# Key slots of 64 in every batch, the first batch loaded ahead of both weights, and a two-way list order, in a fused sliding-window attention and two-layer projection

## The chip, the core and the metric

The kernel runs on one core of one Trainium2 chip. The time is the device time of one execution in microseconds (us). Five engines work beside one another, each on its own queue of instructions in a fixed order: TensorE (PE, with its weight loads as PEld), VectorE (DVE), ScalarE (ACT), GpSimd (POOL) and SyncE (SP). SP and, here, ACT issue the transfers (DMA).

## The reference

```python
# q, k, v: (8 batches, 8 heads, 576 positions, 64); w_in (512, 2048); w_out (2048, 512); all float32
scores = (1.0 / np.sqrt(64)) * np.matmul(q, k.transpose(0, 1, 3, 2))
rel = pos[:, None] - pos[None, :]
mask_plain = (rel >= 0) & (rel < 32)                      # heads 0 to 3
mask_dil = (rel >= 0) & (rel < 128) & (rel % 4 == 0)      # heads 4 to 7
attn = softmax(np.where(mask, scores, -1e9))
x = np.matmul(attn, v)         # heads side by side: (8 * 576 tokens, 512)
h = x @ w_in
out = np.maximum(0.01 * h, h) @ w_out
```

A query sees 32 keys: its own and the 31 before it, or every fourth of the 128 before it. In residue order (positions 0, 4, 8, ..., then 1, 5, 9, ...) a dilated head's 32 keys stand next to one another.

## The kernel before

**Attention.** A *visit* is two heads of one batch, a *unit* is a part of a visit: three units a visit (`unit`, L695 on), so 12 per batch and 96 in all. Scores (L726, L742) multiply a slot of 128 neighbouring keys with 96 queries of both heads, 192 columns a matmul; the queries of the two heads stand on different halves of the partitions, with zeros in the other half (`qbd`). ACT takes exp out of PSUM (L748), DVE multiplies by the mask (L762), and the values matmuls (L796, L806) have ones in half of their stationary columns, so that the same pass gives the values on partitions 0 to 63 and the sums on 64 to 127. ACT makes the reciprocal as exp(-Ln) (L818, L820), and DVE normalises into `xt` (L824), for plain heads in one instruction of 64 partitions per head. Scores rotate over one PSUM bank (`sps0`), values over two (`ops0`, `ops1`). In the first parts of batches 0 and 1, and there alone, the mask is added by a matmul of the identity with a bias (L723), and values and sums are separate matmuls there (L774, L786) on 64 columns of the array.

**Getting q, k and v in.** Batches 0 and 1 are loaded in rows of 1024 bytes, cast to fp16, transposed by PE (L580) and copied into the slots by DVE or ACT (L532, L530); the last 64 positions of these batches come later, as a second part (`load_rest`, L409). Batches 2 to 7 come in pieces of 128 bytes, are cast by POOL (L258), transposed in blocks by DVE (L562, L573), and POOL puts q in place (L567). v is loaded with overlap, since the slots of 128 keys overlap.

**Projections.** A chunk is 384 tokens of a pair of batches. `up` (L835 on) makes 16 blocks of hidden features per chunk (L851, four matmuls of 384 columns each), ACT writes the leaky relu (L862). The first four tiles of 128 tokens are multiplied with w_out plainly, `down` (L892 on; L903, 16 matmuls of 512 columns). All others go in groups of four through `group` (L943 on), which forms 7 products instead of 8 from sums of blocks (sums L979, matmuls of 256 columns L993, evictions L1022 to L1030). These need four sums of blocks of w_out (`weight_sums`, L932).

**The order of the work.** All instructions are tasks of a list scheduler (`_Plan`). Each has a price in us, written by hand, dependences and a priority; `run` (L84) goes forward in time once and takes on each engine the ready task of the lowest priority number. Priorities are due times: `WHEN` and `RANKS` for the attention of each batch, `begins` for the chunks, and the string `FIRST` for the order of the first loads: here `v` and `c` and `b`, `y` are groups of q and k or v of batches 0 and 1, `i` and `o` are slices of w_in and w_out, digits are the last 64 positions. The resulting order is fixed in the program. All loads pass `load` (L248), most on SP. Where the plan leaves PE idle before the first second projection, dummy matmuls of zeros are put in (L1196), and eight at the very start (L1110).

Of the kernel before, what the change touches and what calls it, by code (L numbers as in the profile page):

```python
# [12 lines left out]
ALU = mybir.AluOpType  # L13

WIN = 32
AHEAD, LATE = 5.0, 4.0
WHEN = (-5.0, 15.0, 50.0, 77.0, 112.0, 138.0, 172.0, 200.0)
CON = -1484.5
AFTER = -1495.0
FIRST = "bvbviiii0iiiicoocoyoooooy1"  # L20
RANKS = ((10.0, 6.0), (10.0, 0.5), (15.0, 2.0), (25.0, 2.0))


def _constants():

    ident = np.eye(128, dtype=np.float16)
    p = np.arange(128)[:, None]
    key = p - 32
    c = np.arange(96)[None, :]
    qry = 4 * (c % 24) + c // 24  # L30
    rel = qry - key
    band = (rel >= 0) & (rel < WIN)
    first = band & (key >= 0)
    rel0 = c - p
    d0 = (rel0 >= 0) & (rel0 < WIN)
    c1 = np.arange(48)[None, :]
    rel1 = 96 + c1 - (16 + p)
    d1 = (rel1 >= 0) & (rel1 < WIN)
    rel2 = 96 + c1 - np.where((p < 64) & (p % 4 == 0), 128 + p // 4, p)
    d2 = (rel2 >= 0) & (rel2 < WIN)  # L40
    masks = np.concatenate([first, band, band, d0, d1, d2], axis=1)
    parts = [ident, np.where(masks, 0.0, -60000.0), masks]
    return np.concatenate([x.astype(np.float16) for x in parts], axis=1)


class _Task:
    __slots__ = ("choices", "eng", "lat", "deps", "fn", "prio", "soft", "n", "start", "done",
                 "dur", "left", "ready", "users", "service", "kind", "late")

    def __init__(self, choices, lat, deps, fn, prio, soft, n, kind):  # L50
        self.choices, self.lat, self.fn = choices, lat, fn
        self.prio, self.soft, self.n, self.kind = prio, soft, n, kind
        self.deps = [d for d in deps if d is not None]
        self.eng = self.start = self.done = self.dur = None
        self.left = 0
        self.ready = 0.0
        self.users = []
        self.service = self.late = 0.0


class _Plan:
# [16 lines left out]
    @staticmethod  # L78
    def better_elsewhere(t, eng, at, free):
        end = at + dict(t.choices)[eng]  # L80
        return any(max(free.get(e, 0.0), t.ready) + d < end - 0.02
                   for e, d in t.choices if e != eng)

    def run(self):  # L84
# [3 lines left out]
        def enter(t):  # L88
            for eng, _ in t.choices:
                waiting.setdefault(eng, []).append(t)  # L90

        for t in self.tasks:
            for d in t.deps:
                d.users.append(t)
# [3 lines left out]
        order = []  # L98
        while len(order) < len(self.tasks):
            best = None  # L100
            for eng, cand in waiting.items():
                if not cand:
                    continue
                here = free.get(eng, 0.0)
                if eng == "SP":
                    here = max(here, server - AHEAD)
                could = [t for t in cand
                         if not self.better_elsewhere(t, eng, max(here, t.ready), free)]
                if not could:
                    continue  # L110
                at = max(here, min(t.ready for t in could))
                pick = min(((t.ready + t.soft > at + 1e-9, t.prio, t.n), t)
                           for t in could if t.ready <= at + 1e-9)
                if best is None or (at, pick[1].n) < best[:2]:
                    best = (at, pick[1].n, eng, pick[1])
            at, _, eng, t = best
            for e, _ in t.choices:
                waiting[e].remove(t)
            t.eng, t.start, t.dur = eng, at, dict(t.choices)[eng]
            free[eng] = at + t.dur  # L120
            if t.service:
                begin = max(at + t.dur + 0.9, server)
                server = begin + t.service
                t.done = server + 1.1 + t.late
            else:
# [8 lines left out]
        return order  # L134
# [3 lines left out]
def kernel(  # L138
# [18 lines left out]
    NP = H // 2  # L157
# [5 lines left out]
    TILED = ((0, 0), (1, 0))  # L163
    BY_PE = ((0, 0), (1, 0))
    POOL_MASK = (1,)
    WIDE = (2, 3, 4, 5, 6)
    BLOCKS = tuple(range(16))
    N_UPS = 8
# [20 lines left out]
    NMASK = 288 + 96 + 48 + 48  # L189
    NCON = 128 + 2 * NMASK  # L190
    con = sbuf("con", [128, NCON])
    ident = con[:, 0:128]
    M_PL, M_D0, M_D1, M_D2 = 128, 128 + 288, 128 + 288 + 96, 128 + 288 + 96 + 48
    w_in = sbuf("w_in", [128, NI * DFF])
    w_out = sbuf("w_out", [128, NJ * DM])
    NST, NNAT, NVS, NV, NT, NE, NR, NO, NG = 5, 3, 2, 3, 6, 4, 3, 3, 3
    PAD = 32
    stg = [sbuf(f"stg{i}", [128, 1152], FP32) for i in range(NST)]
    nat = [sbuf(f"nat{i}", [128, 1152]) for i in range(NNAT)]
    vst = [sbuf(f"vst{i}", [128, 2048], FP32) for i in range(NVS)]  # L200
    vp = [sbuf(f"vp{i}", [128, 12 * 128]) for i in range(NV)]
    vd = [sbuf(f"vd{i}", [128, 16 * 128]) for i in range(NV)]
    slots = sbuf("slots", [128, NT * (3 * S + PAD)])
    qbd = [slots[:, i * 2 * S:(i + 1) * 2 * S] for i in range(NT)]
    kt = [slots[:, NT * 2 * S + i * (PAD + S):NT * 2 * S + (i + 1) * (PAD + S)]
          for i in range(NT)]
    ee = [sbuf(f"ee{i}", [128, 384]) for i in range(NE)]
    rc = [sbuf(f"rc{i}", [128, 384], FP32) for i in range(NR)]
# [4 lines left out]
    ones = sbuf("ones", [128, D])  # L213
    turned = [sbuf(f"turned{i}", [128, S]) for i in range(2)]
    wst = [sbuf(f"wst{i}", [128, 2048], FP32) for i in range(1)]
    warm = sbuf("warm", [128, 256])
    t4 = sbuf("t4", [128, 2048])
    pair1 = sbuf("pair1", [128, 1024])
# [5 lines left out]
    tpb = bank("tp", FP16)  # L224
    ops = [bank(f"ops{i}") for i in range(2)]
    hps = [bank(f"hps{i}") for i in range(2)]
    banks = {"S": [bank("sps0")], "O": ops}
    banks["S0"] = banks["S"] + hps[1:]
    banks["O0"] = ops + hps[:1]
    fps = [bank(f"fps{i}") for i in range(2)]  # L230
    tpk = fps[1].bitcast(FP16)

# [3 lines left out]


    def took(n, size):
        for a, ta, b, tb in ((4, 9.0, 128, 15.0), (128, 15.0, 256, 19.0), (256, 19.0, 1024, 48.0),
                             (1024, 48.0, 2048, 85.0)):  # L240
# [4 lines left out]
    def load(queue, dst, src, n, size, deps, prio, slow=1.0):  # L245
        eng = ENG[queue]
        return plan.dma(queue, 0.7 if size == 128 else 0.48, took(n, size) * slow, deps,
                        lambda e: eng.dma_start(dst, src), prio,  # L248
                        LATE if prio > -1500 + len(FIRST) else 0.8 if prio >= AFTER else 0.0)

    def cast(dst, src, n, deps, prio, engines=("POOL",)):
        cost = {"POOL": 0.05 + n * 0.00102, "DVE": 0.08 + n * 0.00056, "ACT": 0.06 + n * 0.00087}
# [8 lines left out]
    def clear(eng, dst, dur, value, prio, deps=()):  # L261
        return add(eng, dur, 0.2, deps, lambda e: ENG[e].memset(dst, value), prio, 0.0, "set")
# [10 lines left out]
    def zeros(n):  # L273
# [3 lines left out]
    t_id = load("ACT", con[:, 0:128], const_d[:, 0:128], 128, 256, [], -1498.95)  # L277
    t_bias = load("ACT", con[:, 128:128 + NMASK], const_d[:, 128:128 + NMASK], 128, 2 * NMASK, [],
                  -1498.5)
    t_con = load("SP", con[:, 128 + NMASK:NCON], const_d[:, 128 + NMASK:NCON], 128, 2 * NMASK, [],  # L280
                 CON)

    t_zero = {}

    def clear_slots(slots, prio, deps):
        for i in slots:
            t_zero[i] = ([clear("DVE", qbd[i][64:128, 0:S], 0.34, 0.0, prio, deps),
                          clear("DVE", qbd[i][0:64, S:2 * S], 0.34, 0.0, prio, deps)],
# [958 lines left out]
```

## Time and profile before

| | |
|---|---|
| time, median of 3 runs | 316.6 us (314.88 to 317.88) |
| span of the profiled execution | 315.0 us, granted TensorE clock 0.994 (the page gives no other time of that execution; its span lies within the three runs) |
| DMA | 51.20 MB, 163395 packets, 140448 of them under 512 B |

Read the profile in this order: the page's busy times and 40 slices of the span (each digit tenths of a slice) tell which engine is full when; the answer by stretches gives the same in us; the chain of waits tells what followed what on the way to the end; the groups by line give instructions (xcount), busy us, mean ns of one, and what their engine waited for just before them. A busy PE is not a PE at its pace: each matmul is counted with its fill and drain, which overlap those of its neighbours.

### The profile page before, as it was taken

To read this page: it belongs to the slowest core of one execution; us is meant where nothing else is said; L and a number is where in the kernel's file an instruction comes from. 1 tells how busy PE (TensorE), PEld (TensorE's weight loads), DVE (VectorE), ACT (ScalarE), POOL (GpSimd) and SP (SyncE) were. 2 spreads that over 40 slices of the span, in tenths; PEclk is the share of its full clock that TensorE was granted. 3 is DMA by queue.
4 is the path that set the end of the run, shared out by engine and by line. 5 is a ranking of instruction groups with operands and counts; after the bars stand their busy time and mean duration, and the time that the engine had idled before them with its cause. 6 is when DMAs were issued, how large, how long until landed. Compare 5 with 4: busy or idle time off the path is not lost.

```text
span 315.0 us, 7276 instructions
## 1 busy us (share of the span) xinstructions
PE 297.0 (94%) x2622; PEld 216.2 (69%) x2622; DVE 222.7 (71%) x453; ACT 231.9 (74%) x534; POOL 133.9 (43%) x175
## 2 busy tenths in 40 slices
PE   7996999799889998899999999999899999999995
PEld 3644554467778786688777777787687777767784
DVE  5844899755988999987979878779956442151172
ACT  3934864589998899789899998699697885454421
POOL 3558655563564767455655747957200000000000
PEclk9999999799999999999999999999999999999999
DMA  7999999999599932899599978796203010130223
GB/s 252 343 332 397 403 295 197 246 174 205 180 173 200 233 60 73 163 188 245 114 220 184 195 184 140 187 182 168 58 10 92 4 34 2 45 91 0 57 79 100
DMA packets 163395, 51.20 MB, mean 163 GB/s; under 512 B 140448, under 2 KB 160800, under 8 KB 163360
## 3 DMA queue, kind: packets, MB, share of 16 engines
q1 hardware_dynamic: 162336, 50.01, 66.6%
q10 hardware_dynamic: 1024, 0.75, 0.8%
q8 instruction: 20, 0.33, 0.4%
q14 instruction: 15, 0.12, 0.1%
HBM read 41.30 MB, written 9.44 MB: 161 GB/s over the span
## 4 chain that ended last, share of the span: by engine, by line
PE 61%; DVE 14%; DMA 7%; SPq 6%; ACT 6%; issue 4%; DVEq 0%; ACTq 0%
PE hps L851 29%; PE fps L993 18%; SPq L248 6%; PE tp L993 6%; DMA wst<-in_moe_w_in_dram 3%; DVE xt L824 3%; ACT gt L862 3%; DMA stg<-in_q_dram 3%; PE ops L806 2%; PE sps L742 2%; DMA stg<-in_k_dram 2%; DVE slots L532 2%; DVE gt L979 2%; DVE ee L762 2%; DVE rest L979 1%
## 5 line engine op out<-in xcount | busy, mean ns | idle before, releaser
L851 PE MATMUL hps<-xt,w_in 128*128 128x384 f16 (+1 forms) x812 | 149.2, 316 | 5.7 <-ACT gt L862 1.9
L862 ACT ACTIVATE gt<-hps 128x384 f16<-128x384 f32 (+1 forms) x203 | 92.3, 461 | 35.9 <-PE hps L851 33.6
L851 PEld LDWEIGHTS <-w_in 128*128 128x128 f16 x832 | 77.0, 98 | 42.6 <-issue 7.7
L993 PEld LDWEIGHTS <-gt 128*128 128x128 f16 x768 | 73.5, 98 | 12.2 <-DVE gt L979 0.7
L824 DVE TENSOR_TENSOR xt<-ops,rc 64x192 f16<-64x192 f32 (+2 forms) x138 | 52.1, 397 | 24.0 <-ACT rc L820 19.3
L567 POOL COPY slots<-turned 64x576 f16<-64x576 f16 x48 | 36.0, 749 | 52.0 <-DVE turned L562 50.4
L818 ACT ACTIVATE rc<-ops 64x384 f32<-64x384 f32 (+1 forms) x94 | 43.5, 464 | 12.9 <-PE ops L806 4.0
L748 ACT ACTIVATE ee<-sps 128x384 f16<-128x384 f32 x92 | 44.7, 485 | 8.6 <-PE sps L742 4.4
L258 POOL CAST nat<-stg 128x576 f16<-128x576 f32 (+1 forms) x53 | 42.0, 816 | 13.0 <-DMA stg<-in_k_dram 6.5
L993 PE MATMUL fps<-w_out,gt 128*128 128x256 f16 x368 | 47.5, 273 | 0.0
L820 ACT ACTIVATE rc<-rc 64x384 f32<-64x384 f32 (+1 forms) x96 | 46.5, 491 | 1.1
L762 DVE TENSOR_TENSOR ee<-ee,con 128x384 f16<-128x384 f16 x79 | 38.4, 492 | 12.5 <-ACT ee L748 12.0
L1030 DVE TENSOR_TENSOR osb<-tp,stg 128x512 f32<-128x512 f32 x14 | 9.6, 686 | 25.0 <-ACT stg L1022 16.8
L742 PE MATMUL sps<-slots 128*128 128x192 f16 x152 | 25.0, 246 | 0.9 <-DVE slots L532 0.8
L258 POOL CAST vd<-vst 128x1024 f16<-128x1024 f32 (+2 forms) x20 | 19.2, 983 | 6.6 <-DMA vst<-in_v_dram 6.4
L742 PEld LDWEIGHTS <-slots 128*128 128x128 f16 x160 | 15.4, 102 | 8.1 <-DVE slots L532 1.4
L1022 ACT COPY stg<-fps 128x512 f32<-128x512 f32 (+1 forms) x26 | 13.9, 534 | 9.4 <-PE fps L993 9.3
L532 DVE COPY slots<-tp 64x128 f16<-64x128 f16 (+7 forms) x43 | 13.6, 333 | 7.2 <-PE tp L580 6.7
L573 DVE STREAM_TRANSPOSE slots<-nat 128x576 f16<-128x576 f16 x24 | 18.0, 762 | 0.7 <-POOL nat L258 0.6
L562 DVE STREAM_TRANSPOSE turned<-nat 128x576 f16<-128x576 f16 x24 | 18.1, 762 | 0.1
L979 DVE TENSOR_TENSOR gt<-gt 128x1024 f16<-128x1024 f16 x21 | 17.2, 838 | 0.8 <-PE fps L993 0.7
L993 PE MATMUL fps<-wst,gt 128*128 128x256 f16 x128 | 16.4, 273 | 0.0
(102 smaller groups left out, 317.6 us busy)
## 6 DMA issues: line engine op xcount, KB each, us to landing
vst<-in_v_dram SPq DMA_DIRECT2D x14, 512.0 KB, 4.8
stg<-in_q_dram SPq DMA_DIRECT2D x48, 144.0 KB, 3.3
stg<-in_k_dram SPq DMA_DIRECT2D x48, 144.0 KB, 2.9
vst<-in_v_dram SPq DMA_DIRECT2D x6, 768.0 KB, 5.6
gt<-in_moe_w_in_dram SPq DMA_DIRECT2D x5, 512.0 KB, 8.3
out_dram<-osb SPq DMA_DIRECT2D x22, 96.0 KB, 2.0
out_dram<-osb SPq DMA_DIRECT2D x44, 48.0 KB, 1.7
out_dram<-osb SPq DMA_DIRECT2D x27, 64.0 KB, 2.6
```

The lines of the kernel that those rows point to most:

```text
L258: ENG[e].tensor_copy(out=dst, in_=src)
L567: lambda e, p0=p0, hh=hh: nc.gpsimd.tensor_copy(out=at(qb, p0, p0 + 64, hh * S + o, *od), in_=at(xb, p0, p0 + 64, i, *id_)), prio)
L742: nc.tensor.matmul(st[:, 192 * i:192 * i + 192], ka, qa, start=not by_pe, stop=i == 1 or not by_pe)
L748: lambda e: nc.scalar.activation(out=et, in_=st[:, 0:384], func=AF.Exp, scale=SCALE), prio + 0.1)
L762: ENG[e].tensor_tensor(out=io, in0=io, in1=mk, op=ALU.mult)
L818: lambda e: nc.scalar.activation(out=r_out, in_=r_in, func=AF.Ln), prio + 0.2)
L820: lambda e: nc.scalar.activation(out=r_out, in_=r_out, func=AF.Exp, scale=-1.0),
L824: nc.vector.tensor_tensor(out=dst, in0=at(ot, p0, p1, c, *i_), in1=at(rt, p0, p1, c, *i_), op=ALU.mult)
L851: nc.tensor.matmul(ht[:, 0:n], at(w_in, 0, 128, i * DFF + j // 2 * 256 + j % 2, [2, 128]), at(xt[m % 2], 0, 128, i * 1152 + x0 + x, [1, n] ...
L862: lambda e: nc.scalar.activation(out=gt[c % NG][:, j * n_c + x:j * n_c + x + n], in_=ht[:, 0:n], func=AF.Prelu, alpha=0.01),
L979: lambda e: ENG[e].tensor_tensor(out=dst, in0=a, in1=b, op=op),
L993: nc.tensor.matmul(bk[:, x:x + HN], tl[:, off + j * step:off + j * step + 128], rhs(j), start=first and x == 0 and j == 0, stop=j == HJ - ...
```

## The change

The program is rewritten around slots of 64 keys; the projections keep their matmuls.

- A visit has two units instead of three (`unit`), 64 in all. A unit makes five score matmuls of at most 96 columns, one per slot of 64 keys of *both* heads: the stationary operand is now k (two heads on a diagonal, zeros elsewhere, written once), and q is dense. A second pass with a block matrix of ones (`block_ones`) into the same PSUM bank gives the sums on all partitions, a third gives the values. So Ln, its exp and the normalisation run once per unit on 128 partitions and 288 columns. A unit takes two banks in turn out of three (`sps0`, `ops0`, `ops1`); batch 0 has one or two more. All units of batches 0 and 1 have the mask as a bias on PE; the others have it on DVE as before.
- x is kept in residue order in all batches, 288 columns a unit; w_in's rows are loaded so that a block of 128 rows is one visit's two heads. Chunks change with it: chunk 0 is two thirds of batch 0, half of chunk 1 is its last third.
- v has no overlap any more, is loaded on 64 partitions per head, and two casts put it on the slot's diagonal. In late batches q is dense (plain visits are transposed straight into the slot), and k is copied onto the diagonal by POOL or ACT.
- `FIRST` now loads all of batch 0 (q and k of the dilated group, last positions, q and k of the plain group, v of both), then w_in, then batch 1 and w_out mixed, then the mask table. Part of batch 0's loads is issued by ACT. Units of an early batch wait for its last positions too.
- `run` makes eight passes: forward as before, then backward from the end; each task's priority becomes its latest start, except first loads and dummies, and the pass of the shortest plan is kept. Second projections of plain tiles, sums and stores keep their form. Dummies stop at the first `up`.

```diff
-AHEAD, LATE = 5.0, 4.0
-FIRST = "bvbviiii0iiiicoocoyoooooy1"
+AHEAD, LATE = 5.0, 3.0
+PASSES = 8
+FIRST = ('q01 r0 q00 v01 v00 w0 w1 w2 w3 w4 w5 w6 w7 q11 r1 v11 w8 w9 q10 w10 w11 v10 '
+         'w12 w13 w14 w15 c')
...
+        for i in range(PASSES):
+            order, end = self.forward()
+            if best is None or end < best:
+                best = end
+                keep = [(t, t.eng, t.start, t.dur, t.done) for t in order]
+            begin = self.backward(end)
+            for t in self.tasks:
+                if not t.fixed:
+                    t.prio = begin[t.n]
...
+        by_pe = b < EARLY
+        p_bank, v_bank = (banks[(bank_at[0] + i) % len(banks)] for i in range(2))
+        bank_at[0] += 2
+        p_old, p_users = grab(p_bank)
+        v_old, v_users = grab(v_bank)
...
+            for i, (s, qd, qx, c, w, _, _) in enumerate(steps):
+                nc.tensor.matmul(p_bank[:, c:c + w], slot(tn, KB + 128 * s, 0, 128, [1, 128]),
+                                 slot(tn, qx, 0, 128, *qd), start=first or not by_pe,
+                                 stop=i == len(steps) - 1 or not by_pe, skip_group_check=True)
...
+        t_sum_ = add("PE", 0.2, 0.25, [t_m, t_e, t_id], second(p_bank, lambda s: block_ones),
+                     prio, 0.4, "z")
+        t_v = add("PE", 0.2, 0.25, [t_m] + v_in[b, vi] + v_old,
+                  second(v_bank, lambda s: slot(tn, VB + 128 * s, 0, 128, [1, 128])), prio, 0.4, "v")
...
+        t_l = add("ACT", 0.06 + 288 * 0.00085, 0.2, [t_sum_] + r_old,
+                  lambda e: nc.scalar.activation(out=rt, in_=p_bank[:, 0:288], func=AF.Ln), prio)
+        p_users.append(t_l)
...
+                    got.append(move(slot(tn, x, p0, p1, [128, 9], [1, D]),
+                                    at(xk, p0, p1, 0, [D, 9], [1, D]), S, [tk] + old, prio,
+                                    ("POOL", "ACT")))
...
+            made = [cast(slot(tn, VB + hh, 64 * hh, 64 * hh + 64, [128, 9], [2, D]),
+                         at(vs, 64 * hh, 64 * hh + 64, j * S, [D, 9], [1, D]), S,
+                         lv[hh][j] + old, prio, ("POOL", "ACT") if b < EARLY else ("POOL",))
+                    for hh in range(2)]
...
+            src = dram(moe_w_in, heads_of(vi)[0] * D * DFF + x, [DFF, 64], [2 * D * DFF, 2], [1, 1024])
...
-        if u.kind == "D":
+        if u.kind in "UD" and u.kind:
             break
```

More of the change, by code (lines that the diff above doesn't have):

```diff
@@ L124, in run @@
                 t.done = server + 1.1 + t.late
+                touched.add("SP")
             else:
@@ L132, in run @@
                     enter(u)
-        order.sort(key=lambda t: (t.start, t.n))
-        return order
+                    touched.update(e for e, _ in u.choices)
+            multi = set(touched)
+            for e, cand in waiting.items():
+                if e not in multi and any(len(c.choices) > 1 for c in cand):
+                    multi.add(e)
+            for e in multi:
+                cached.pop(e, None)
+        order.sort(key=lambda t: (t.start, t.n))
+        return order, max(t.done for t in order)
```

1160 lines of the change are left out of this document (514 added, 646 removed).

## The prediction, made before the changed kernel was run

> **What bounds the kernel now.** I read the page's parts 1 and 2, then the stages, then the chain of waits for the pace of the matmuls, then the groups kept apart by shape.
>
> ```profile
> PE 297.0 (94%) x2622; PEld 216.2 (69%) x2622; DVE 222.7 (71%) x453; ACT 231.9 (74%) x534; POOL 133.9 (43%) x175
> ...
> PE   7996999799889998899999999999899999999995
> DVE  5844899755988999987979878779956442151172
> ACT  3934864589998899789899998699697885454421
> ```
>
> ```profile
> 0.00:35.00 35.00, 29.69 (x243) 16.43 (x244) 21.56 (x67) 19.91 (x50) 20.86 (x39) 1.00 0.99 338
> 35.00:60.00 25.00, 21.51 (x186) 11.71 (x185) 23.58 (x57) 14.83 (x38) 13.51 (x18) 0.98 0.96 264
> 60.00:100.00 40.00, 37.69 (x366) 29.08 (x365) 29.58 (x59) 35.79 (x94) 22.10 (x29) 0.97 0.97 197
> 100.00:140.00 40.00, 38.16 (x354) 28.71 (x352) 38.28 (x66) 35.32 (x80) 24.31 (x29) 1.00 0.72 144
> 140.00:300.00 160.00, 158.79 (x1383) 120.91 (x1381) 101.99 (x193) 123.71 (x269) 53.18 (x62) 1.00 0.52 112
> ```
>
> Columns: stretch, length, busy time of PE, PEld, DVE, ACT, POOL, granted clock, DMA share, GB/s. PE looks full everywhere, but a lone matmul counts with its whole pipeline. The chain gives the true pace:
>
> ```profile
> 30.17 1.14 PE hps L851 x7
> 31.30 0.17 PE sps L742 x2
> ...
> 31.63 0.22 PE tp L580 x4
> ...
> 33.90 0.20 PE ops L796 x8
> ...
> 34.95 1.73 PE fps L903 x8
> ...
> 37.45 0.17 PE ops L806 x4
> ```
>
> So a matmul of 384 columns takes 0.162 us, 192 0.083, 128 0.056, 96 0.042, 48 0.025, 512 0.216; one of 256 0.109 (eight in 0.87). Counts times these paces: first projection 704 x 0.162 + 128 x 0.082 = 124.5; second 896 x 0.109 + 64 x 0.216 = 111.5; attention 35.7 (160 x 0.083 and 64 x 0.042 for the scores, 256 x 0.042 and 128 x 0.025 for the values, 5.7 for the bias and the early half-array matmuls); transposes 80 x 0.056 = 4.5. That is 276 us of work in a span of 315.0, so 39 are lost, and the same count by stretch puts them: 16.5 before 35 us (one chunk of the first projection is done by then), 6.6 from 35 to 60, 5.9 from 60 to 100, 3.1 from 100 to 140, 2.6 from 140 to 300, 4.4 in the tail. PE is the bound, and only lost time can be won. In the first stretch the DMA is full (0.99); from 35 to 60 and from 100 to 140 DVE is (23.6 of 25, 38.3 of 40), and around 60 to 100 ACT (35.8 of 40). Three runs' median is 316.6; the profiled span is 315.0, and I add that 1.6 at the end.
>
> ```profile
> L762 DVE TENSOR_TENSOR ee<-ee,con 128x384 f16<-128x384 f16 x79 | 38.4, 492 | 12.5 <-ACT ee L748 12.0
> L824 DVE TENSOR_TENSOR xt<-ops,rc 64x192 f16<-64x192 f32 x88 | 27.8, 344 | 13.3 <-ACT rc L820 12.7
> L824 DVE TENSOR_TENSOR xt<-ops,rc 64x384 f16<-64x384 f32 x36 | 19.7, 547 | 9.5 <-ACT rc L820 5.6 <-PE ops L796 1.8 <-PE hps L851 1.5
> ```
>
> **The change, part by part.**
>
> *PE work.* 64 units instead of 96, each with three passes (scores, sums, values) of five matmuls. A dilated unit has 96, 96, 80, 80 and 32 columns: 2 x 42 + 2 x 36 (between the rows for 48 and 96) + 25 = 181 ns; a plain one 193 or 186. 64 x 3 x 0.186 = 35.7. The bias of the 16 early units, 3 matmuls of 0.18 us together, is 2.9; 72 transposes 4.0. That is 42.6 against 40.2: +2.4. For 32 columns the nearest rows are 48 (25 ns, taken) and, as array time alone, a third of 96 (14 ns): with the low end +0.7, with all 144 of them at the 42 of 96 columns +4.9.
>
> *ACT, per late batch.* Before, 12 units x (485 + 487 + 516 ns, rows L748, L818, L820) = 17.9. Now 8 x (0.50 + 0.41 + 0.44): 400 columns by row L748, 288 between the rows for 192 (332 and 365) and 384. That is 10.8, and, by the list of instructions, 23 of 48 copies of k at about 0.6 (row L530, 580) add 2.3: 13.1, less by 4.8.
>
> *DVE, per late batch.* Before, 12 masks x 0.492, 12 normalisations x 0.344 and 6 x 0.547, 8 transposes x 0.762: 19.4. Now 8 masks x 0.51, 8 normalisations x 0.45 (128 partitions at once, between L824's 192 and 384 columns), the same transposes, a few copies of 64 columns: 14.2, less by 5.2.
>
> *POOL, per late batch.* 8 casts x 0.834 stay; 8 copies x 0.749 and 4 casts of v (4.2) become 8 casts of v on 64 partitions at 0.834 (a cast costs by columns, not by partitions: 64x512 took 854 ns, 128x512 612), two copies of q and 4 or 5 of k: 17 to 18 against 16.9. POOL has 43%, so this hides; if POOL were full each batch would pay 1.
>
> *DMA.* v goes in without overlap: 1.2 MB a batch, not 1.8. The mask table grows by 0.3 MB, and it comes last. SP issues about as many loads as before; at most eight transfers are in flight, and each load waits for the one eight places ahead.
>
> *The start.* In the trace of before DVE casts the first half at 3.97 and exp starts at 8.04. Now ACT casts it, and ACT first issues seven loads, the last of which, by the waits in the build, waits for q's second half (the SP load that waits for that one in the trace of before issues at 5.36). So casts from 6.0, three of 0.62; every unit also needs the last 64 keys, so their casts, transposes and six small moves stand ahead of the first exp: about 11. From there ACT paces: 8 x 1.35 + two casts of v + one move = 12.6, so the batch is done near 24, and this is all 576 tokens where before had 384 at 17. The weights follow 3.5 MB of the batch: 7.8 MB at the page's 252, 343, 332 and 397 GB/s land at 25. Half of the first chunk (2 of 4 head pairs) runs under the attention; the rest ends near 32.5, 1.5 of it for the eight evictions (0.49 each) ahead of the two banks that the later ones use. Useful by then: 10.4 + 5.9 + 2.9 = 19.2; lost 13.3, against 16.5. Ends: 10 (nothing but the landing of the weights) and 20 (attention four us later and its evictions in series).
>
> *The dummy matmuls* now stop at the first ups, not at the first second projections. The eight dummies at the very start ran at 0.43 us for 512 columns, half the later pace; if PE fell back to that in the gaps under batch 0's attention, the first 32 ups would take 5 us more, of which about 3 would show. In the trace of before, waits of up to 1.9 us after the start changed no pace, so I take 0 and keep the 3 inside the start's upper end.
>
> *32 to 60.* The w_out slices land at 47 as before. The list gives PE the 16 half ups of chunk 1 (5.3), six units, transposes and six quarters of second projections (0.87): 16.5 us of work for 15.5 to 48, so little is lost, then the rest of chunks 1 and 2 (15.7) is there. The last units of batch 1 stand behind the quarter that needs the last slice but one; the two other plain tiles (6.9) cover them, without that cover 3 us. DVE has 15 us of casts, moves and normalisations in these 17. I take 3, ends 1 and 8, against 6.6.
>
> *60 to 140.* DVE and ACT lose a quarter of their load per batch, so the waits of 9.0 should shrink; I take 3, ends 0.5 and 9 (nothing gained). From 140 on 2.6 and the tail 4.4 stay: the products and their sums are unchanged.
>
> *Sum.* 278.4 + 13.3 + 3 + 3 + 2.6 + 4.4 = 304.7, plus 1.6: 306.
>
> *A rule to weigh.* The row: pairs of weight load and matmul of 96 columns run every 42 ns, of 128 every 56, while a load is shown as 98 ns. The Trainium skill, "TensorE: Matmul & The Clock Gate", section "Back-to-back issue gap", says that in a real kernel such pairs of 128 columns come every 81 ns or so, since the load counts too. The trace here does not agree.
>
> **The rivals.**
>
> *The three shared banks become the bound (slower).* One bank now holds a unit from scores to Ln, another from values to normalisation, and late batches rotate three. In the trace of before, means of the late units: scores to end of exp 1.44, to end of mask 1.39, to values 1.14, to Ln 0.85, Ln 0.41: 5.2; values to the end of normalisation 2.9. So 8.1 us of bank, 2.7 a unit, under the 4.1 that PE needs per unit. Against it: that margin. For it: each hold now contains three in-order queues' waits, and the longest waits in the trace are 3.6, 6.8 and 3.9. 48 late units from 50 on and the 59 us that follow the last values (256 to 315): at 12.9 us of bank a unit the time is that of before, at 13.5 it is 50 + 216 + 59 + 1.6 = 327.
>
> *The middle gives nothing:* in-order waits, not DVE's load, made the 9.0; for it, ACT is as full as DVE. 304.7 + 6 + 1.6 = 312.
>
> *The early batch gives nothing (the change doesn't do what it says):* the weights land 3 us later, the gain of 3.2 at the start is gone: 310. For it: the DMA is full in either order.
>
> *All waits but the start's and the tail's close:* 278.4 + 13.3 + 1 + 1 + 1 + 4.4 + 1.6 = 301, less with a start of 11: 299.
>
> *Weight loads set the pace.* If the 960 small matmuls took the 98 ns of the weight load row instead of 37, they would cost 58 us more: 364. Against it, every row of small matmuls. By the 81 ns of the Trainium skill (the section named above) an estimate is 42 more, 348.
>
> **How the numbers follow.** About 1% is what a measurement of this kernel can tell from no change. Forecast 0.42 (own range 302 to 311), banks 0.20, middle 0.18, start 0.10, all waits closed 0.07, weight loads 0.03. Faster by over 1% (under 313.4): 0.41 + 0.12 of the middle's + 0.09 + 0.07 = 0.69. Within 1%: 0.01 + 0.06 + 0.01 + 0.04 of the banks' = 0.12. Slower: 0.16 + 0.03 = 0.19. The range from 296 to 322 leaves out about 0.03 below and 0.16 above.
>
> **What would show it.** The first ups near 18 and the first second projections of 512 columns before 40; fewer gaps on PE from 35 to 60; DVE's total near 185 and ACT's near 222; PE's small matmuls at 42 ns or less; scores not waiting for Ln or normalisation of an earlier unit. Wrong would be: DVE or ACT still full from 60 to 140 with PE waiting; PE waiting on xt after 60; first exp later than 13.

## The result, and the profile after

The changed kernel takes 353.8 us (median of 4 runs, 352.7 to 357.7), the kernel before, on the same chip, 315.8: a ratio of 1.123 [1.115, 1.131]. The forecast was 306, with a range of 296 to 322. The profiled execution took 357.7 us with a span of 355.8.

The page of the changed kernel, with the lines that answer to those shown of before:

```profile
PE 302.8 (85%) x2883; PEld 223.9 (63%) x2883; DVE 186.9 (53%) x329; ACT 207.9 (58%) x479; POOL 131.8 (37%) x189
...
PE   4788789766669769698959969999999999999996
...
DVE  4484447744643855497265386685373353115072
ACT  1697666545746466346738737777667684553521
...
PEclk9599999999978998989989989999999999999999
DMA  7899899799999799789989986501200301011133
```

DVE's 187 us and ACT's 208 are near the forecast of 185 and 222. But from slice 8 to 24 (of 8.9 us each) PE has holes, and no compute engine is full there for more than a slice; only the DMA's row stays high. By stretches:

```profile
0.00:35.00 35.00, 25.45 (x245) 16.88 (x245) 18.36 (x39) 21.24 (x49) 16.36 (x29) 0.85 0.92 272
35.00:60.00 25.00, 19.66 (x222) 13.76 (x223) 12.90 (x26) 16.62 (x44) 14.18 (x19) 1.00 1.02 272
60.00:100.00 40.00, 29.33 (x304) 21.11 (x302) 23.39 (x39) 23.92 (x61) 20.39 (x31) 1.00 1.05 149
100.00:140.00 40.00, 30.35 (x260) 20.99 (x259) 21.81 (x38) 21.98 (x49) 24.08 (x34) 0.87 1.23 154
140.00:300.00 160.00, 145.63 (x1443) 110.65 (x1442) 91.22 (x158) 101.72 (x232) 56.84 (x77) 0.97 0.56 99
```

From 60 to 100 us the DMA moves 149 GB/s at a share of 1.05, where the kernel before moved 197 at 0.97: divided by the share, the DMA carries 30% less (142 against 203 GB/s). A part of that is another mix of packets, since run 1 below, with the loads of the changed kernel and its tiles moved back, has 181. The chain of waits shows what such a hole is made of:

```profile
97.12 4.48 DMA stg<-in_k_dram
101.60 0.03 issue
101.62 0.04 POOLq L337
101.67 0.08 issue
101.75 0.68 POOL nat L337
102.42 0.02 issue
102.45 0.04 DVE turned L542
...
103.15 0.75 DVE ee L699
103.90 0.04 issue
103.94 0.51 PE sps L705 x5
104.45 1.28 PE hps L748 x4
```

The load of k is one of batch 3. POOL casts it, DVE transposes it (L542), and behind that transpose, in DVE's fixed order, stands the mask (L699) of a unit of batch 2, for which PE waits: 3.5 us. Batch 2 needs nothing of that load. And the four matmuls of 384 columns after the hole take 1.28 us, 0.32 each, twice the 0.162 of before: the granted clock is 0.50 from 104 to 108 us, with a mean of 0.87 from 100 to 140.

The mask and normalisation groups, answering to L762 and L824, cost 0.49 to 0.53 us (forecast 0.51) and 0.55 (forecast 0.45):

```profile
L729 DVE TENSOR_TENSOR xt<-ops,rc 128x288 f16<-128x288 f32 x41 | 22.6, 552 | 16.5 <-ACT rc L718 15.3 <-PE ops L705 1.2
...
L699 DVE TENSOR_TENSOR ee<-ee,con 128x384 f16<-128x384 f16 x24 | 12.5, 529 | 7.1 <-ACT ee L695 7.0
L699 DVE TENSOR_TENSOR ee<-ee,con 128x416 f16<-128x416 f16 x24 | 11.8, 492 | 11.1 <-ACT ee L695 10.8
```

So two things were to be found: why the loads are slower, and why an engine's order puts a late load ahead of work that doesn't need it.

*Why slower.* From issue to landing the 144 KB loads of q and k, the same in both kernels, take 2.9 to 3.3 us before and 4.5 to 4.6 after. First the DMA part of the kernel before, then of the changed one (KB each, median us to landing):

```profile
stg<-in_q_dram SPq DMA_DIRECT2D x48, 144.0 KB, 3.3
stg<-in_k_dram SPq DMA_DIRECT2D x48, 144.0 KB, 2.9
```

```profile
stg<-in_q_dram SPq DMA_DIRECT2D x48, 144.0 KB, 4.6
stg<-in_k_dram SPq DMA_DIRECT2D x48, 144.0 KB, 4.5
```

The trace's records of single packets say it more sharply: 110,592 packets of 128 bytes in both, mean 12.9 ns before (91% of them 13), 17.1 after (median 13, a quarter at 20 or more, a tenth at 28 or more). One thing differs in where they go: `con` grew from 2176 to 4032 bytes a partition, and all tiles behind it moved. `stg` and `vst` started on a multiple of 128 bytes before, 64 off one after.

*Why in that order.* The change also lowered the planner's prices of a packet: 128 bytes from 15 to 9.5 ns, 256 from 19 to 13.3, 1024 from 48 to 41 (function `took`), and its allowance for landing from 4 to 3 us. The trace before has 13, 18 and 52. The start times that the planner in each kernel computes, against the issue in the run, for every 48th load or store on SP (us):

```
number on SP        48      96     144     192   end
before   plan     50.3    99.6   137.0   177.8   307.9
         run      52.3   100.0   141.9   184.2   315.0
after    plan     39.4    70.1   100.1   129.8   300.6
         run      59.7   105.1   149.4   188.0   355.8
```

The plan of before is 0.4 to 6.4 us ahead of its run at these loads, that of after 20 to 58.

### The profile page after: what moved, and what is told of

Same layout as the page of the kernel before. It is cut to its first block, busy times and chain, and to the rows that moved or that the text cites. A ratio compares the mean times of both kernels' runs of the same rounds, so it can differ in the third digit from the quotient of the medians.

```text
span 355.8 us, 7577 instructions
## 1 busy us (share of the span) xinstructions
PE 302.8 (85%) x2883; PEld 223.9 (63%) x2883; DVE 186.9 (53%) x329; ACT 207.9 (58%) x479; POOL 131.8 (37%) x189
## 4 chain that ended last, share of the span: by engine, by line
PE 46%; DMA 23%; SPq 18%; POOL 4%; issue 4%; DVE 3%; ACT 2%; POOLq 0%; DVEq 0%
PE hps L748 20%; SPq L325 18%; PE fps L892 15%; DMA stg<-in_k_dram 12%; PE tp L892 5%; DMA stg<-in_q_dram 4%; DMA vst<-in_v_dram 4%; DMA gt<-in_moe_w_out_dram 3%; PE ops L705 2%; POOL nat L337 1%; POOL slots L337 1%; PE sps L705 1%; PE ops L688 1%; PE ops L892 1%; POOL slots L350 1%
## 5 line engine op out<-in xcount | busy, mean ns | idle before, releaser
L337 POOL CAST slots<-vst 64x576 f16<-64x576 f32 x60 | 52.2, 875 | 19.7 <-DMA vst<-in_v_dram 10.1
L892 PE MATMUL fps<-w_out,gt 128*128 128x256 f16 x368 | 49.4, 280 | 0.0
L705 PEld LDWEIGHTS <-con 128*128 128x128 f16 x320 | 20.1, 100 | 24.7 <-issue 21.1
L542 DVE STREAM_TRANSPOSE turned<-nat 128x576 f16<-128x576 f16 x24 | 18.2, 770 | 31.2 <-POOL nat L337 22.8
L699 DVE TENSOR_TENSOR ee<-ee,con 128x384 f16<-128x384 f16 (+1 forms) x48 | 24.3, 511 | 18.1 <-ACT ee L695 17.9
L729 DVE TENSOR_TENSOR xt<-ops,rc 128x288 f16<-128x288 f32 x41 | 22.6, 552 | 16.5 <-ACT rc L718 15.3
L688 PEld LDWEIGHTS <-slots 128*128 128x128 f16 x320 | 18.9, 100 | 19.0 <-issue 14.7
L718 ACT ACTIVATE rc<-rc 128x288 f32<-128x288 f32 x64 | 27.8, 442 | 1.0
L716 ACT ACTIVATE rc<-ops 128x288 f32<-128x288 f32 x40 | 16.3, 410 | 15.2 <-PE ops L705 15.0
L348 ACT COPY slots<-turned 64x512 f16<-64x512 f16 (+1 forms) x23 | 15.2, 661 | 15.7 <-DVE turned L542 15.6
L695 ACT ACTIVATE ee<-ops 128x384 f16<-128x384 f32 (+1 forms) x40 | 19.9, 501 | 7.4 <-PE ops L688 7.2
L350 POOL COPY slots<-turned 64x576 f16<-64x576 f16 (+2 forms) x33 | 19.7, 603 | 7.2 <-PE sps L688 4.0
L705 PEld LDWEIGHTS <-slots 128*128 128x128 f16 x320 | 17.9, 99 | 2.8 <-issue 0.9
```

What stands on the lines that cost most here:

```text
L337: ENG[e].tensor_copy(out=dst, in_=src)
L350: ENG[e].tensor_copy(out=dst, in_=src)
L688: nc.tensor.matmul(p_bank[:, c:c + w], slot(tn, KB + 128 * s, 0, 128, [1, 128]), slot(tn, qx, 0, 128, *qd), start=first or not by_pe, stop ...
L695: lambda e: nc.scalar.activation(out=et[:, 0:n], in_=p_bank[:, 0:n], func=AF.Exp, scale=SCALE), prio)
L699: lambda e: nc.vector.tensor_tensor(out=et[:, 0:n], in0=et[:, 0:n], in1=con[:, table:table + n], op=ALU.mult), prio)
L705: nc.tensor.matmul(at(dst, 0, 128, o, *od), lhs(s), et[:, c:c + w], start=i == 0, stop=i == len(steps) - 1, skip_group_check=True)
```

## The experiments

Theory A: the place of the tiles. Theory C: the plan's prices. Rivals: B, the form and number of the loads; D, SP's own work; E to H, the start. All ratios are to the kernel before on the same chip.

**1. Tiles back on a multiple of 128**

```diff
-    con = sbuf("con", [128, NCON])
+    con = sbuf("con", [128, NCON + 32])
```

> One edit to the changed kernel: the constants' tile `con` is 64 bytes per partition longer (unused), so that every SBUF tile behind it (stg, vst and all others that loads write into) starts 64 bytes later, on a multiple of 128 bytes, as it does in the kernel before; in the changed kernel these tiles start 64 bytes off such a multiple. Order and instructions are the same. Theory A, the place in SBUF: a packet of 128 bytes written across a boundary of 128 costs more; packets of 128 bytes return from a mean of 17 ns to 13, of 256 from 26 to 18, the waits of POOL's casts for q and k (56 us in the changed kernel) fall below 20, and the time falls from 354 to between 305 and 330. Rival B, the form of the loads (v on 64 partitions, ten small loads a batch instead of three, another order of q and k): packets stay at 17 and 26 ns and the time within 1% of 354.

343.8 us, 1.085 [1.079, 1.090]: 10 us gained. Packets of 128 bytes are back at 13.0 ns, of 256 only at 21.1; POOL still waits 36 us for q and k. Theory A holds for a part: the time is outside its range of 305 to 330, the packets of 256 bytes and POOL's waits did not fall as far as it says. Rival B explains none of the 128-byte packets.

**2. The kernel before, tiles moved by 64 bytes** (the same line in the kernel before)

> The reverse edit, to the kernel before: `con` 64 bytes per partition longer, so that stg, vst and the tiles behind them start 64 bytes off a multiple of 128, as in the changed kernel. Theory A: packets of 128 bytes go from 13 ns to about 17, of 256 from 18 to about 26; the DMA's packet time grows by some 40 us of 210, and the time from 316 to 325 to 350, as far as the loads then come late. Rival B: packets stay at 13 and 18 ns, 316 us within 1%.

330.3 us, 1.043 [1.038, 1.048]; packets 17.4 and 23.7 ns; landing 5.1 and 4.6 us. As Theory A says.

**3, 4. The old prices, with and without the padding**

```diff
-        for a, ta, b, tb in ((4, 7.0, 128, 9.5), (128, 9.5, 256, 13.3), (256, 13.3, 1024, 41.0),
-                             (1024, 41.0, 2048, 81.0)):
+        for a, ta, b, tb in ((4, 9.0, 128, 15.0), (128, 15.0, 256, 19.0), (256, 19.0, 1024, 48.0),
+                             (1024, 48.0, 2048, 85.0)):
```

> The changed kernel with `con` padded by 64 bytes as in the first experiment, and the planner's prices of a load's packets put back to those of the kernel before (128 bytes 15 ns, 256 bytes 19, 1024 bytes 48, against 9.5, 13.3 and 41 in the change; the trace has 13, 18 and 46 to 52). No instruction changes, only their order. Theory C, the plan's prices: with loads priced too low the plan puts the casts and copies of a coming batch where its loads have not landed, and on POOL, in order, they hold up the work of the batch at hand; with the old prices POOL's waits for q and k (36 us in the padded kernel) fall below 12, PE's lost time after 60 us (37) below 15, and the time from 344 to between 308 and 322. Rival B, the form of the loads (24 loads a batch on SP instead of 19): SP is busy 18 to 19 us of 20 in either order, 344 within 1.5%.

> The changed kernel with the old prices of packets alone, tiles still 64 bytes off. Theory C: most of what the third experiment gains on the padded kernel is gained here too, 354 to between 318 and 337 (packets of 128 bytes still 16 to 17 ns, so the plan's 15 is nearly honest). Rival B: 354 within 1.5%.

With the padding 322.0 us, 1.019 [1.014, 1.023]; without it 336.9, 1.067 [1.062, 1.071]. The same work in another order (a few copies go to another engine, and five more dummies run): 22 and 17 us. PE's lost time from 60 us on falls from 41 in the padded kernel to 20, not below 15. POOL's waits for q and k did not fall as expected (32 us):

```profile
POOL nat L337 <- DMA stg<-in_k_dram: 22.6, 10, 5.7
POOL slots L337 <- DMA vst<-in_v_dram: 17.6, 14, 6.9
POOL nat L337 <- DMA stg<-in_q_dram: 9.5, 5, 4.6
```

They cost less, since what now stands behind them is due later. An engine's total wait was the wrong gauge; what counts is what is queued behind the wait.

**5. The kernel before with the low prices** (the reverse edit)

> The kernel before with the change's low prices of packets (9.5, 13.3 and 41 ns) and nothing else; its plan then ends at 304 instead of 308. Theory C: its order puts work ahead of the loads that it needs, and the time grows from 316 to between 321 and 335, with POOL's waits for loads (18 us) above 30. Rival: the prices hardly move an order that due times set: 316 within 1%.

334.0 us, 1.059 [1.054, 1.063]. POOL's waits for loads are 43 us (18 in the kernel before):

```profile
POOL vd L258 <- DMA vst<-in_v_dram: 15.5, 8, 4.4
...
POOL nat L258 <- DMA stg<-in_k_dram: 12.7, 10, 3.7
POOL vp L258 <- DMA vst<-in_v_dram: 8.7, 6, 3.1
...
POOL nat L258 <- DMA stg<-in_q_dram: 6.5, 6, 2.0
```

The prices alone cost the kernel before 18 us. Its plan had ended 4 us earlier with them.

**6. v's loads on ACT**

```diff
+        queue = "ACT" if b >= EARLY else queue
...
-                lo = load("SP", at(vs, p0, p0 + 64, 0, [D, 18], [1, D]),
+                lo = load(queue if b >= EARLY else "SP", at(vs, p0, p0 + 64, 0, [D, 18], [1, D]),
```

> On top of the padded kernel with the old prices (322 us): the loads of v of batches 2 to 7, 48 of them, are issued by ACT instead of SP. Theory D, the issuing queue: SP is busy 18 to 19 us of every 20 from 60 to 200 us and issues each late load just in time; without a third of its loads it falls to 13 to 16 and the time from 322 to between 312 and 318. Rival, plan and landing: the loads come no earlier, since the order and the DMA set them, and ACT pays some 5 us a batch for issuing: 321 to 330.

336.6 us, 1.068 [1.059, 1.078]. SP's busy time falls further than expected, to 8 to 14 of 20 us between 60 and 200, and the time grows by 15, more than the rival says. The loads gain nothing here, but ACT now spends 37 us on issuing instead of 6.5, so this run alone can't rule Theory D out; the next one speaks to it.

**7. Honest prices of issuing**

```diff
-AHEAD, LATE = 5.0, 3.0
+AHEAD, LATE = 5.0, 4.0
...
-        t = plan.dma(queue, 0.7 if size == 128 else 0.55, took(n, size) * slow, deps,
+        t = plan.dma(queue, 0.85 if size == 128 else 0.65, took(n, size) * slow, deps,
```

> On top of the padded kernel with the old prices (322 us): the plan's price for issuing a load goes from 0.70 and 0.55 us to 0.85 and 0.65 (means of the trace), and its allowance for landing from 3 to 4 us, as in the kernel before. Only the order changes. Theory C (what is left is still a plan that runs ahead of the loads: it ends at 305 where the run has 321): 314 to 319. Theory D (SP's own work is the limit): 321 to 325.

317.2 us, 1.005 [1.001, 1.008]: Theory C again. SP is as busy as in the third kernel (18 to 19 of 20 us from 40 to 200), yet its issuing all but leaves the chain that ends last, here by engine in the third kernel and in this one:

```profile
PE 38%; SPq 20%; DMA 18%; DVE 7%; POOL 6%; issue 5%; ACT 5%; ACTq 0%; POOLq 0%; DVEq 0%
```

```profile
PE 69%; DMA 12%; ACT 7%; DVE 6%; issue 2%; POOL 1%; SPq 1%; DVEq 0%; POOLq 0%; ACTq 0%
```

So SP's work as such is not the limit, and Theory D falls.

**8. One pass instead of eight** (`PASSES = 1`, on the third kernel)

> On top of the padded kernel with the old prices (322 us): one forward pass with the due times as priorities, as the kernel before does it, instead of eight passes in two directions. The plan then ends at 310 instead of 305. If the two-way order is worth on the chip what it is in the plan: 326 to 330. Rival: the two-way order puts each task at its latest start and so has no slack against a late load; then one pass is as fast or faster: 314 to 322.

323.1 us, 1.027 [1.019, 1.034], beside 322.0: of the 5 us that the plan gives the two-way order, the chip shows 1, within the intervals. Neither expectation held. With the low prices one pass was not tried; the kernel before is planned in one pass and loses 18 us by them (run 5), so the damage does not need the two-way order.

**9. Prices as measured** (on 7: 256 bytes 21 ns, 1024 52, 2048 98, longer ones 23.7 bytes a ns)

> On top of the kernel with honest issuing prices (317 us): the other packets get the durations that the traces of the rewritten kernel show (256 bytes 21 ns, 1024 bytes 52, 2048 bytes 98, and 23.7 instead of 25.6 bytes a ns above). The plan then ends at 311 instead of 307. Only the order changes. Theory C (each step of honesty in the plan gains while the plan still runs ahead; at load 48 it was 12 us ahead of the run): 311 to 316, PE's lost time from 35 to 100 us below 8 (9.7). Rival: what is left of the plan's lead costs nothing, 316 to 320.

315.4 us, 1.000 [0.997, 1.003], its interval overlapping that of run 7. PE's lost time from 35 to 100 us is 9.6, not below 8; 140 to 220 fell from 3.0 to 1.5. Load 48 is planned for 49.4 and issued at 59.9, number 144 for 126.9 and 137.6: the lead is now 10 to 14 us. The plan's prices of computing lie below the trace too (for the mask 0.38 us against 0.49 to 0.53, for the normalisation 0.40 against 0.55); no run changes them.

**10. The kernel before with honest issuing prices**

> The kernel before with the issuing prices of 0.85 and 0.65 us instead of 0.70 and 0.48, nothing else; its plan ends at 309 instead of 308. Its run already follows its plan within 7 us, so Theory C expects little: 316 within 1%. Rival: any plan gains from honest prices, 310 to 313.

316.5 us, 1.004 [1.002, 1.006]: as Theory C says of a plan that its run already follows.

**11 to 15. The start**

```diff
-FIRST = ('q01 r0 q00 v01 v00 w0 w1 w2 w3 w4 w5 w6 w7 q11 r1 v11 w8 w9 q10 w10 w11 v10 '
+FIRST = ('r0 q01 q00 v01 v00 w0 w1 w2 w3 w4 w5 w6 w7 q11 r1 v11 w8 w9 q10 w10 w11 v10 '
...
-                load_v(b, int(step[2]), tick(), "ACT" if b == 0 else "SP")
+                load_v(b, int(step[2]), tick(), "SP")
```

On the third kernel, then on the ninth:

> On top of the padded kernel with the old prices (322 us): at the start the loads of batch 0's last 64 positions go ahead of those of q01, and the two small loads of v that ACT issued go to SP, so that ACT is free to cast when the first q lands. Theory E, the start: the last positions' k landed at 12.0 us and held the first exp until 15.0; now first exp at 11 to 13, and the time falls by 2 to 3, to 319 to 320. Rival: the weights' landing and the casts of v set the end of the start, the time stays within 1 us of 322.

> As the run with measured prices, and the start with the last positions' loads first and ACT free of v's loads. Theory E: 1 to 2 us below that run. Rival: the same within 1 us, since the loads of w_in stand behind the same small loads, eight in flight, and land no earlier.

320.7 us, 1.017 [1.011, 1.024] beside 322.0, and 314.4, 0.998 [0.995, 1.001] beside 315.4: 1 us each, within the intervals. The first exp moves only from 15.0 to 14.3, because POOL still casts k's last rows, now first in the list, at 11.9, when they have landed. In the second of these orders a dummy matmul (L1098 at 18.86 us) is put into the bank that then holds the scores of a unit of batch 0 (`hps0`), so the values of that unit are other ones; the work is the same. The next version leaves out dummies after the fourth unit's scores:

```diff
+    n_s = 0
     for t, u in zip(pe, pe[1:]):
-        if u.kind in "UD" and u.kind:
+        n_s += u.kind == "s"
+        if n_s > 4 or u.kind in "UD" and u.kind:
             break
```

> The version with measured prices, padded tiles and the last positions' loads first, and now no dummy matmul after the fourth unit's scores, so that none is written to a bank that a unit holds. Theory C with all corrections: 312 to 316, the rewritten kernel then level with the kernel before or up to 1% faster; PE's lost time 17 to 18 before 35 us, 2 to 5 to 60, 7 to 8 to 140. Rival: without the dummies' warmth PE is slower at the start, 316 to 319.

319.3 us, 1.009 [1.005, 1.013], 5 us over the version with those dummies and outside both expectations. The granted clock from 10 to 20 us is 0.66 there and 0.83 with them, but the profiles don't tie this or the 5 us to the three dummies left out. In the version with them, these run at 17.3 and 18.9 us, when PE's matmuls are back at full pace (from 16.8 on). Without them the start is late before that: POOL casts k's last rows at 12.4 instead of 11.6, and the first scores with q come at 14.7 instead of 13.0. Of the 6 us more that PE loses in the profiled execution, some 4 are lost from 140 to 220 us. What makes the 5 us stays open.

On that version, w_in ahead of v (`r0 q01 q00 w0 w1 w2 w3 v01 v00 w4 ...`), and batch 0's v in two loads instead of six (`if g == 0 or b == 0:`):

> On top of the version with all corrections: the first four slices of w_in are loaded ahead of batch 0's v instead of behind it. Theory F, the weights' place: w_in is issued from 13.4 us on, behind 18 loads; issued some 6 us earlier, the first ups start earlier (22.5 us) and the time falls by 1 to 3. Rival G, attention's chain: the values of batch 0 then wait for v, the first ups stay at 22 us or later, and the time stays or grows by up to 3.

> On top of the version with all corrections: batch 0's v of the dilated group comes in two loads of 288 KB instead of six of 32 and 128 KB. It then stands in the order of the plain group, so the values of that one group in that one batch are other ones; the work is the same. Theory H, eight loads in flight: with small loads eight carry too little, the DMA moves 215 to 240 GB/s in the first 16 us; with four fewer it moves 250 or more, w_in issues some 2 us earlier, and the time falls by 1 to 2. Rival: the packets of 256 bytes cost as much as is gained, no change within 1 us.

The first gives 317.3, 1.005 [1.003, 1.008]: w_in is issued from 6.3 us on, yet the first ups start at 27.9 instead of 24.0. The last rows of k are now cast at 15.5 instead of 12.4, and the first exp comes at 18.3 instead of 15.2. So the mechanism of Theory F fails: attention's own chain sets the first ups. The profiled execution took 322.0, 5 us over the median, and the median, 2 us below the base's, has an interval that overlaps the base's; the time decides nothing. The second gives 316.2, 1.003 [0.999, 1.006], 3 us below its base, the intervals just touching; but w_in is issued only 0.7 us earlier, and the DMA moves 242 GB/s from 10 to 20 us (219 in the base; this profiled execution took 321.1). The time speaks for Theory H, whose signs (2 us and 250 GB/s) did not come: the mechanism is not shown.

**16. Control: the kernel before, tiles moved by 128 bytes** (`NCON + 64`)

> Control to the shift by 64 bytes: the kernel before with `con` 128 bytes longer, so that the tiles behind it move but stay on multiples of 128. Theory A: packets of 128 bytes at 13 ns, 316 us within 1%. Rival (any move of these tiles costs, by another neighbour or bank): 16 ns or more, 325 to 333 us.

318.6 us, 1.011 [1.006, 1.016]. Packets of 128 bytes stay at 13.3 ns, those of 256 go from 18.0 to 20.8. So the rival falls, since packets of 128 bytes don't pay for this move; those of 256 do. Either a packet pays when it crosses a multiple of its own size, or when it crosses one of 256; these placements don't tell the two apart.

**17, 18. The ninth kernel with tiles on multiples of 256 and of 512** (`NCON + 96`, `NCON + 224`)

> The version with measured prices (315.4 us, tiles on odd multiples of 128) with `con` 192 instead of 64 bytes longer, so that stg and vst start on multiples of 256. The control, 128 bytes further, had left packets of 128 bytes at 13 ns and raised those of 256 from 18 to 21; the mended versions have 21 too. Theory A, widened (a packet pays when it crosses a boundary of its own size): packets of 256 bytes fall to 18 ns, the DMA's packet time by 4 us, the time by 1 to 3, to 312 to 314.5. Rival B (v's form on 64 partitions costs those 3 ns): 21 ns stay, 315.4 within 1.

> The same with `con` 448 bytes longer: stg and vst start on multiples of 512. If the boundary is the packet's own size up to 256, the same as on 256, 18 ns and 312 to 314.5; if 512 counts too, packets of 1024 bytes fall from 55 to 52 ns and the time by up to 1 more. Rival B: 21 ns, 315.4 within 1.

314.5 us, 0.997 [0.994, 0.9995], and 313.9, 0.995 [0.993, 0.997]: the only versions whose interval lies below the kernel before, by 0.3 to 0.5%. All placements side by side, mean ns of a packet in the trace:

```
kernel                      stg starts at   128 B   256 B   1024 B   4096 B
before                        402   x 128    12.9    18.0    52.5    173
before, 64 bytes further      402.5 x 128    17.4    23.7    55.9    178
before, 128 bytes further     403   x 128    13.3    20.8    53.6    175
after                         416.5 x 128    17.1    26.3    57.8    174
after, 64 bytes further       417   x 128    13.0    21.1    54.9    175
prices measured, on 256       418   x 128    12.8    18.2    52.0    169
prices measured, on 512       420   x 128    12.9    18.5    52.1    176
```

512 instead of 256 changes nothing that can be measured; rival B's 64 partitions cost nothing here either (18.2 ns). The Trainium skill, "DMA: Bandwidth & Descriptors", section "How a descriptor splits into AXI transactions", says of reading that a descriptor is cut into transactions that begin on multiples of 256 bytes, and that one which starts off such a multiple can take one more. Here it is the written side that moved, the addresses read are the same, and the trace agrees in part: 64 bytes off, every second packet of 128 crosses a multiple of 256, the median stays 13 and a quarter take 20 or more; 128 bytes off, none crosses, and the mean is 13.3. But the slow packets come in bursts. Of the groups of 64 packets of 128 bytes that start one after another in the changed kernel, a third have over 60% above 13 ns, up to 98%, and its packets of 4 bytes (16 with each transfer) go from a mean of 9.0 to 11.8 ns. So packets that cross nothing are held up as well. That the place makes the difference is shown, a rule for the single packet is not.

## Why the prediction was wrong, point by point

PE's lost time by stretch, counted as in the prediction (useful work 276 us before, 279 in all the others):

```
                          to 35   35-60   60-140   140-220   from 220
before                     16.5     6.5      8.9       0.5       6.5
forecast                   13.3     3        3         2.6 and 4.4
after                      19.0     6.7     27.0      20.4       4.0
3: padded, old prices      17.8     4.2      6.3       9.6       4.4
9: prices as measured      19.2     4.1      7.8       1.5       4.3
18: and tiles on 512       17.4     3.6      7.3       0.4       4.4
```

The stretches of the last kernel, columns as before:

```profile
0.00:35.00 35.00, 28.02 (x262) 17.58 (x263) 19.50 (x40) 21.29 (x50) 18.19 (x32) 0.95 0.86 278
35.00:60.00 25.00, 22.58 (x275) 16.77 (x273) 14.16 (x29) 18.50 (x52) 13.62 (x17) 1.00 0.93 276
60.00:100.00 40.00, 36.08 (x352) 26.38 (x351) 28.04 (x42) 24.99 (x64) 27.07 (x33) 1.00 0.84 166
100.00:140.00 40.00, 38.73 (x406) 30.03 (x405) 33.79 (x54) 30.92 (x70) 26.73 (x39) 1.00 0.88 169
140.00:300.00 160.00, 159.81 (x1527) 122.19 (x1525) 90.60 (x153) 106.58 (x241) 54.94 (x77) 1.00 0.47 100
```

- *DMA (failed).* "The mask table grows by 0.3 MB, and it comes last", and no price was put on it. Its tile grows too and moves every tile behind it, and this step was put at nothing; packets of 128 and 256 bytes cost 17 and 26 ns instead of 13 and 18. Price: 10 us in the plan of the change, 15 under the old prices, 14 put into the kernel before.
- *60 to 140, and 140 on (failed).* "The waits of 9.0 should shrink; I take 3", and "from 140 on 2.6 and the tail 4.4 stay". The orders were compared as if each would run as planned; that the plan's prices of loads had been lowered below the rows of the trace was passed over. 27 us were lost from 60 to 140, and 20 from 140 to 220. The granted clock (0.87 from 100 to 140, 0.96 to 180, 0.91 to 220) gives an estimate: at most 40 x (0.13 + 0.04 + 0.09) = 10 of these went to a slower pace, the rest to waits. Of the signs of being wrong, DVE and ACT full did not come (23 and 24 of 40 us from 60 to 100); PE waiting on xt did, 4.7 us of first projections after 60 us. Price: 17 to 22 us for the packets, 5 for issuing and landing, 2 for the rest. What is left of the middle in the last kernel, 7.3, is closer to the 9.0 of the rival "the middle gives nothing" than to the 3.
- *Sum of the corrections.* 353.84 - 10.08 (place) - 21.76 (old prices) - 4.76 (issuing) - 1.86 (measured prices) - 1.46 (512) = 313.92. These are differences of medians one after another, so they add up by construction; the last two steps are at or within the intervals.
- *The start (failed in size).* 13.3 forecast, 17.4 to 19.2 in the orders above. The first exp came at 16.3 instead of 11, which is the sign "later than 13". ACT's casts started at 9.3, not 6.0, and POOL could cast the last rows of k only at 13.65, when they had landed behind the other small loads. Where ACT was freed (run 11) its casts did start at 6.0, yet those rows were cast at 11.9 and exp came at 14.3: the term that was too small is the landing of k's last rows. First ups at 22.5, not 18, and the first second projections of 512 columns at 43.5, not before 40. The upper end of 20 held the size.
- *The dummies.* "I take 0 and keep the 3 inside the start's upper end": 0 held. From 20 to 60 us, the first ups at 22.5 and what follows, the granted clock is 1.00 without them. The slow pace (0.50 from 10 to 15 us) comes before the first ups, where dummies still run, after PE has waited 5.3 us for the first cast.
- *Right.* PE's work, 279 against 278.4: matmuls of 96, 80 and 32 columns every 42, 35 and 29 ns (forecast 42, 36, 25). The Trainium skill's 81 ns ("TensorE: Matmul & The Clock Gate", "Back-to-back issue gap") does not agree with these rows either (128 columns come every 56 ns), and the rival of the weight loads falls; that 353.8 lies between its 348 and 364 is chance. DVE 187 (185), ACT 208 (222), POOL 132 to 141 (not full). 35 to 60: 2.7 to 4.6 once tiles and prices were mended (3). The rival of the three banks falls as well, for the last kernel: there, scores wait once from 60 to 140, 1.5 us, for a normalisation. In the changed kernel they did wait for normalisations after 60 us, 9.6 us in six waits, with the same banks; the order and the late loads made the difference.

In the last kernel 7.4 us are between the forecast's span (304.7) and the run's (312.1): 4.1 at the start, 4.3 from 60 to 140, 0.6 more each in work and from 35 to 60, 2.2 less later. At 91 to 98 us the chain runs through DVE's sums of blocks (L878, 0.65 to 1.26 us each), which the change left to DVE alone; before, POOL was a choice and took one of them. That was not tried by itself.

## What to carry to other kernels

A list order is only as good as its prices: hold each price of a transfer against the trace, and print the plan's time of some late load beside its issue in the run; a plan that runs 20 us ahead is already wrong, and an optimistic one costs more than it promises. Where a tile grows, look where the tiles behind it come to lie: keep those that small packets are written to on multiples of 256 bytes, where packets of 128 and 256 bytes took least in both kernels. Fillers that write to memory must be known to whatever hands that memory out.

## What the runs showed of the hardware

- Writing small packets to SBUF pays for the place: 64 bytes off a multiple of 128, 128-byte packets go from a mean of 13 ns to 17, and 256-byte ones from 18 to 24 to 26; on an odd multiple of 128 the former show 13.3 and the latter 21. Packets of 4096 bytes show 169 to 178 ns in all the placements of the table.
- After the hole of 3.5 us shown above matmuls ran at half pace (0.32 us for 384 columns instead of 0.162, granted clock 0.50 from 104 to 108 us): here a late load cost PE's clock as well. After a hole of 2.1 us before, at 94.8 us, they ran at full pace.
- SP was busy 18 to 19 us of 20 issuing loads in nearly all versions of the rewritten kernel, those of 354 us and those of 314 alike. Giving a third of its late loads to ACT gained nothing: ACT then spent 37 us on issuing instead of 6.5, and the time grew by 15.
